# Order of issue alone: a planner that keeps VectorE and ScalarE apart by PSUM bank, with a newly searched table of ranks

## The chip, the core and the metric

The kernel runs on one core of one Trainium2 chip. The metric is device time in microseconds (us) of one execution, and less is better. The engines are TensorE (PE, with its weight loads as PEld), VectorE (DVE), ScalarE (ACT), GpSimd (POOL) and SyncE (SP), which here issues every DMA.

## The reference

The output is the sum of three terms for a sequence of S = 2048 tokens of width D = 576: the input itself, a spectral filter of the normalized input, and a mixture-of-experts layer with 64 experts, 32 heads and one choice in each head.

```
xn = layernorm(x)                                     # over the 576 columns
A  = irfft2(rfft2(xn) * (w_r + 1j * w_i))             # 2-D, over tokens and columns
q  = xn @ w_q                                         # 32 heads, 2 * 128 columns each
s1, s2 = q[..., :128] @ k1.T, q[..., 128:] @ k2.T     # 8 scores each
e  = argmax(s1) * 8 + argmax(s2)                      # one expert in each head
B  = sum over heads of gelu(xn . u[e]) * v[e]
out = x + A + B
```

A softmax over a single choice is 1, so the gate of the reference falls away.

## The kernel before

**The spectral branch.** Tokens are numbered n*16 + t, with n on the partitions. `ln(t, n)` normalizes blocks of tokens, `folds(t)` adds and subtracts mirrored columns on POOL and DVE, and `dft128(t)` does the transform of length 128 on PE. Its result is split into a high half in float16 (ACT copies it out of PSUM) and a residue (DVE subtracts the copy from the same PSUM data). The arrays `AB` and `ABL` hold both halves. Then sixteen frequency groups g pass through `d_fwd(g)` (columns), `s_fwd(g)` (length 16, two groups at a time), `s_mul(g)` (the filter, four products on DVE per pair, then POOL and ACT) and `s_inv(g)`, which writes `AB` and `ABL` again. `d_inv(t)` and `fin(t)` finish sixteen token blocks: `d_inv` brings the columns back (PE, then ACT's copy `es`, DVE's `eo`, and POOL's three operations that make `y`), and `fin` does the last length-128 transform plus the product with the experts' v on PE, adds the input on DVE and issues the store.

**The expert branch.** `fold_part(b, s)` multiplies the query weights by the keys while they stream in (32 loads of 576 KB into five buffers `w`), `fold_end` and `fold_last` turn the product into the tables `MU` and `MUL`. For eight blocks r of two token tiles, `x_t(r)` prepares the input, `scores(r)` multiplies it by `MU` and `MUL` (28 matmuls), `route(r)` finds the best choice of each head, and `combine(r)` makes the coefficients, which PE transposes and ACT copies into `CAT` for `fin`. `scores(r)` writes two PSUM banks, one for each token tile. ACT reads columns 448 to 511 of each bank for the gelu (two instructions named `act`), and DVE reads columns 0 to 447 of both banks for the maximum (`mx`) and for the comparison with it (the first write of a `w` buffer). So there ACT and DVE read the same banks, and neither needs the other's result. In `s_inv` ACT makes two copies (`AB` and `ABL`) from the same banks, and DVE's two residues each need one of them.

**What sets the order.** The kernel text is recorded, not issued: each call on an engine becomes an operation of a `_Plan`, with a cost from a table of formulas, a latency, and its dependencies. Up to 900 ns of matmuls of one stage on one PSUM tile are one operation. `forward` then plays a list scheduler: again and again it takes the engine that can start soonest, and on it, of the operations that can start at that time, the one with the smallest number in the table `RANK` (1308 numbers, one for each recorded operation). The same pass hands out PSUM banks to tiles, of which at most `LIMIT` of each kind are open at once. The resulting total order is the order in which the program is issued, engine by engine. The library below the kernel adds the semaphores: PSUM is one tensor called `banks`, and two instructions of different engines on the same bank are put one behind the other in the order in which they are issued, reads too. In the kernel before, the planner doesn't know of that last rule for two reads. [...]

Two more names occur below: `KP` is a small matrix of key differences that POOL makes from `kT` once at the start, and `rr` and `mv` hold the statistics of the normalization. `A` and `t` in the profile are the buffers of `folds` and `d_inv` (`A2_*`, `t1_*`), `yh` also that of `es`, and `MT` those of the routing. All engine calls go through one helper line, so that every row of the profile says L528; the changed file is ten lines longer, and the same helper is L538 there.

## Time and profile before

| | |
|---|---|
| times shown | 226.74, 227.78 and 229.1 us, median 227.78 us |
| profiled execution | span 226.4 us from its first to its last instruction; the page has no other time for it, so it stands 0.3 us below the fastest run shown and 1.4 us below the median |
| PE busy | 198.3 us (88%) |
| DVE busy | 195.3 us (86%) |
| POOL busy | 150.8 us (67%) |
| ACT busy | 135.2 us (60%) |
| DMA moved | 43.43 MB |

Times in the profile are in us unless ns is said. A row of the timeline has the start, the duration, the engine, the line, the operation, the names out<-in, the shape, the count of merged instructions, and in brackets the idle time of the engine before it with what ended it. A row of the view of waits has the waiting engine, what it waited for, and the total, the count and the longest. The view by windows has, for a stretch of the span, its length and then the busy time and count of PE, PEld, DVE, ACT and POOL, the granted PE clock, the DMA share and GB/s.

### The profile page before, as it was taken

To read this page: it belongs to the slowest core of one execution; us is meant where nothing else is said; L and a number is where in the kernel's file an instruction comes from. 1 tells how busy PE (TensorE), PEld (TensorE's weight loads), DVE (VectorE), ACT (ScalarE), POOL (GpSimd) and SP (SyncE) were. 2 spreads that over 40 slices of the span, in tenths; PEclk is the share of its full clock that TensorE was granted. 3 is DMA by queue.
4 is the path that set the end of the run, shared out by engine and by line. 5 is a ranking of instruction groups with operands and counts; after the bars stand their busy time and mean duration, and the time that the engine had idled before them with its cause. 6 is when DMAs were issued, how large, how long until landed. Compare 5 with 4: busy or idle time off the path is not lost.

```text
span 226.4 us, 5987 instructions
## 1 busy us (share of the span) xinstructions
PE 198.3 (88%) x2287; PEld 136.1 (60%) x2287; DVE 195.3 (86%) x423; ACT 135.2 (60%) x294; POOL 150.8 (67%) x217
## 2 busy tenths in 40 slices
PE   0197959999997999899888999999899999999984
PEld 0185536877675367584464665645566767788762
DVE  1979899997769789763999999999999999999843
ACT  2388877888397797949577577545483332242420
POOL 3889887842097829418668585459794977586880
PEclk9999999999999699999999999999999999999999
DMA  6999999979999995533334322200200002223234
GB/s 209 413 430 410 406 409 408 409 254 380 377 385 402 321 356 141 174 99 107 100 114 153 94 80 61 69 4 0 62 3 0 0 3 104 106 110 154 104 115 148
DMA packets 14572, 43.43 MB, mean 192 GB/s; under 512 B 1872, under 2 KB 4688, under 8 KB 14160
## 3 DMA queue, kind: packets, MB, share of 16 engines
q1 hardware_dynamic: 14544, 43.05, 52.0%
q8 instruction: 18, 0.29, 0.6%
q14 instruction: 10, 0.08, 0.1%
HBM read 38.33 MB, written 4.72 MB: 190 GB/s over the span
## 4 chain that ended last, share of the span: by engine, by line
PE 48%; DVE 34%; issue 7%; POOL 4%; ACT 4%; DMA 2%; DVEq 0%; ACTq 0%; POOLq 0%
PE banks L528 48%; DVE MT L528 8%; DVE w L528 6%; DVE t L528 6%; DVE XN L528 3%; POOL t L528 2%; DVE mx L528 2%; DVE A L528 2%; DVE AB L528 2%; DMA XN<-in_x_dram 2%; DVE st L528 1%; POOL A L528 1%; DVE ABL L528 1%; DVE rr L528 1%; ACT yh L528 1%
## 5 line engine op out<-in xcount | busy, mean ns | idle before, releaser
L528 PE MATMUL banks<-MU,xT 128*128 128x512 f16 x192 | 47.5, 379 | 1.1 <-DVE t L528 0.9
L528 POOL TENSOR_TENSOR xT<-xf,xT 128x512 f16<-128x512 f32 (+1 forms) x32 | 26.2, 819 | 16.6 <-ACT xT L528 14.2
L528 POOL TENSOR_TENSOR y<-t,t 128x289 f32<-128x289 f32 x32 | 22.6, 727 | 20.6 <-DVE t L528 20.3
L528 PE MATMUL banks<-c,AB 128*128 128x145 f16 (+1 forms) x384 | 35.2, 227 | 0.0
L528 POOL TENSOR_TENSOR A<-t 128x145 f32<-128x145 f32 (+2 forms) x48 | 31.2, 665 | 5.3 <-DVE t L528 3.1
L528 PEld LDWEIGHTS <-AB 128*128 128x128 f16 x384 | 32.2, 121 | 3.5 <-issue 1.4
L528 PEld LDWEIGHTS <-xT 128*128 128x128 f16 x224 | 20.6, 99 | 22.2 <-issue 2.1
L528 POOL TENSOR_TENSOR t<-XN 128x289 f32<-128x289 f32 x32 | 24.0, 770 | 8.8 <-DVE A L528 4.1
L528 ACT ACTIVATE yh<-banks,sc 128x580 f32<-128x580 f32 x16 | 11.9, 744 | 23.8 <-PE banks L528 16.9
L528 POOL TENSOR_TENSOR yh<-y,yh 128x578 f16<-128x578 f32 x16 | 21.9, 1377 | 5.4 <-ACT yh L528 4.5
L528 DVE SCALAR_TENSOR_TENSOR t<-banks,wx,Wt 128x578 f32<-128x578 f32 x32 | 24.1, 807 | 0.5 <-PE banks L528 0.4
L528 PE MATMUL banks<-A,c 128*128 128x288 f32 x64 | 21.8, 422 | 1.5 <-POOL A L528 0.9
L528 PE MATMUL banks<-Rs,yl 128*99 128x128 f32 x64 | 11.2, 305 | 13.5 <-ACT Rs L528 13.4
L528 PE MATMUL banks<-w,KP 128*32 128x288 f32 x256 | 22.0, 441 | 0.8 <-DVE mm__94 L528 0.8
L528 DVE TENSOR_TENSOR AB<-banks,AB 128x512 f16<-128x512 f32 x32 | 21.4, 675 | 1.3 <-ACT AB L528 0.7
L528 PE MATMUL banks<-c,ABL 99*128 99x289 f16 (+1 forms) x64 | 18.6, 291 | 1.4 <-DVE t L528 1.0
L528 ACT ACTIVATE AB<-banks 128x512 f16<-128x512 f32 x32 | 18.6, 587 | 2.0 <-PE banks L528 1.9
L528 PE MATMUL banks<-Rs,A 128*128 128x128 f32 x128 | 19.0, 298 | 0.0
L528 PEld LDWEIGHTS banks<-Rs,A 128*128 128x128 f32 x128 | 17.1, 209 | 2.5 <-issue 1.4
L528 PEld LDWEIGHTS banks<-Rs,yl 128*99 128x99 f32 x64 | 8.3, 180 | 16.6 <-ACT Rs L528 15.5
L528 DVE TENSOR_REDUCE MT<-w 128x128 bf16<-128x896 bf16 (+1 forms) x16 | 18.1, 1139 | 0.0
L528 ACT ACTIVATE ABL<-banks 99x256 f16<-99x256 f32 x32 | 12.0, 379 | 9.7 <-PE banks L528 9.6
(124 smaller groups left out, 433.3 us busy)
## 6 DMA issues: line engine op xcount, KB each, us to landing
w<-in_wq_dram SPq DMA_DIRECT2D x32, 576.0 KB, 7.0
xf<-in_xT_dram SPq DMA_DIRECT2D x16, 320.0 KB, 3.7
Wt<-in_W_dram SPq DMA_DIRECT2D x8, 578.0 KB, 6.1
out_dram<-XN SPq DMA_DIRECT2D x14, 288.0 KB, 2.1
XN<-in_x_dram SPq DMA_DIRECT2D x3, 1154.0 KB, 10.6
s<-in_s_dram SPq DMA_DIRECT2D x16, 192.0 KB, 3.4
XN<-in_x_dram SPq DMA_DIRECT2D x2, 577.0 KB, 4.6
c<-in_c_dram SPq DMA_DIRECT2D x1, 868.5 KB, 9.8
```

What stands on the lines that cost most here:

```text
L528: fn(*[x.place() if isinstance(x, _Ps) else x for x in args], **{k: x.place() if isinstance(x, _Ps) else x for k, x in kw.items()})
```

## The change

The change is to the planner and its table alone. No call in the body of the kernel is edited, so that each instruction of the program is issued as before, on the same engine, at another place.

Each operation outside PE now lists the PSUM banks of the tiles that it touches (`bk`). While it plans, `forward` keeps for each such bank the planned end of every access, with its engine (`seen`). An operation can start no sooner than the end of each earlier access of another engine to one of its banks. And the 1308 ranks are others. The old ranks were the positions of a finished order; the new ones are keys without such a trend, from which the scheduler makes an order.

```diff
 RANK = (
-    2, 13, 11, 15, 48, 86, 12, 14, 6, 4, 3, 5, 1, 53, 51, 54, 58, 7, 0, 8, 10, 9, 18, 21, 24, 20, 16, 23, 29,
...
+    115, 134, 157, 175, 296, 353, 133, 169, 298, 382, 628, 84, 987, 21, 253, 200, 170, 295, 126, 380, 249,
...
 class _Op:
     __slots__ = ("shape", "tiles", "eng", "calls", "cost", "lat", "deps", "succ", "stage", "pre", "port",
-                 "held", "opens", "after")
+                 "held", "opens", "after", "bk")
...
-            op.tiles, op.port = tiles, port
+            op.tiles, op.port, op.bk = tiles, port, []
...
             if isinstance(x, _Ps):
                 name = x.tile
+                if eng != "tensor":
+                    op.bk += [(name, int(b)) for b in np.flatnonzero(mask) if (name, int(b)) not in op.bk]
...
                 if o.port and port > t:
                     t = port
+                for b in o.bk:
+                    for x, u in seen.get(b, ()):
+                        if x != e and u > t:
+                            t = u
...
-        used, port = {k: 0 for k in LIMIT}, 0.0
+        used, port, seen = {k: 0 for k in LIMIT}, 0.0, {}
...
             if o.port:
                 port = free[e]
                 stale |= {"vector", "gpsimd"}
+            for b in o.bk:
+                seen.setdefault(b, []).append((e, free[e] + o.lat))
+                stale |= {"vector", "scalar"}
```

The sequence of stages stays what it was: a stage is at most some operations earlier or later on its engine. Three places show how it moved.

**ACT, around the gelu of the first block.** `xf` and `xT` belong to `x_t`, `t2` with `wm` to a load of filter weights, `A2` to `d_fwd`, `yh` and `yl` to `s_mul`, and `act_0` is the gelu of `scores(0)`, with the table load that it needs in front. Before:

```order
L528 ACTIVATE A2_2_100<-banks_66 128x578
L528 ACTIVATE A2_3_101<-banks_66 128x578
L528 ACTIVATE t2_0_106,wm_81<-Wt_2_113 128x1156
L528 ACTIVATE yh_1_137<-y_1_135 128x578
L528 ACTIVATE yh_0_136<-y_0_134 128x578
L528 ACTIVATE xT_1_92<-xf_0_123 128x640
L528 ACT_TABLE_LOAD
L528 ACTIVATE act_0_126<-banks_66,gs_88 128x64 x2
L528 ACTIVATE yl_1_105<-yh_1_137 128x396
L528 ACTIVATE xT_1_92<-xf_1_124 128x640
L528 ACTIVATE yl_0_104<-yh_0_136 128x396
```

And now:

```order
L538 ACT_TABLE_LOAD
L538 ACTIVATE act_0_126<-banks_66,gs_88 128x64
L538 ACTIVATE xT_1_92<-xf_0_123 128x640
L538 ACTIVATE t2_0_106,wm_81<-Wt_2_113 128x1156
L538 ACTIVATE A2_3_101<-banks_66 128x578
L538 ACTIVATE yh_0_136<-y_0_134 128x578
L538 ACTIVATE yh_1_137<-y_1_135 128x578
L538 ACTIVATE xT_1_92<-xf_1_124 128x640
L538 ACTIVATE yl_0_104<-yh_0_136 128x396
L538 ACTIVATE A2_2_100<-banks_66 128x578
L538 ACTIVATE yl_1_105<-yh_1_137 128x396
L538 ACTIVATE xf_0_123<-xf_0_123,bx_87 128x640
```

The table load and the first gelu now stand ahead of the other work of that place, and the second gelu, which followed the first at once, comes after the last row shown. In the order of the whole program the two used to stand on both sides of DVE's `mx`; now the first is ahead of it and the second behind both of DVE's reads.

**POOL, at the start of the program.** `t1` from `XN` and `A2` are the folds of the first token tiles, `rr` from `mv` their statistics, and `KP` from `kT` the key differences. Before:

```order
L528 TENSOR_TENSOR t1_0_96<-XN_67 128x289 x2
L528 TENSOR_TENSOR t1_1_97<-XN_67 128x289
L528 TENSOR_SCALAR rr_84<-mv_85 128x2
L528 TENSOR_TENSOR A2_0_98<-t1_0_96 128x145
L528 TENSOR_TENSOR t1_1_97<-XN_67 128x289
L528 TENSOR_TENSOR A2_1_99<-t1_1_97 128x145
L528 TENSOR_TENSOR KP_73<-kT_69 128x2x7 x4
```

And now:

```order
L538 TENSOR_TENSOR KP_73<-kT_69 128x2x7 x4
L538 TENSOR_TENSOR t1_0_96<-XN_67 128x289 x2
L538 TENSOR_TENSOR t1_1_97<-XN_67 128x289
L538 TENSOR_SCALAR rr_84<-mv_85 128x2
L538 TENSOR_TENSOR A2_0_98<-t1_0_96 128x145
L538 TENSOR_TENSOR t1_1_97<-XN_67 128x289
```

The four operations on `KP` moved ahead of the first folds. On the DMA queue the load of `kT` moved from third to second place, between the first two loads of `XN`.

**POOL, at the end of the program.** `t1` from `yh` is the first of the three operations of a `d_inv`, the two `A2` from `t1` are the others, and `MT` from `MT` is the low half of a block's coefficients in `combine`. Before:

```order
L528 TENSOR_TENSOR MT_79<-MT_79 128x2x64
L528 TENSOR_TENSOR A2_1_99<-t1_1_97 128x287
L528 TENSOR_TENSOR t1_0_96<-yh_0_136 128x2x144
L528 TENSOR_TENSOR A2_0_98<-t1_0_96 128x289
L528 TENSOR_TENSOR t1_1_97<-yh_1_137 128x2x144
L528 TENSOR_TENSOR A2_0_98<-t1_0_96 128x287
L528 TENSOR_TENSOR A2_3_101<-t1_1_97 128x287
L528 TENSOR_TENSOR t1_0_96<-yh_0_136 128x2x144
L528 TENSOR_TENSOR A2_3_101<-t1_1_97 128x289
L528 TENSOR_TENSOR A2_2_100<-t1_0_96 128x289
L528 TENSOR_TENSOR A2_2_100<-t1_0_96 128x287
```

And now:

```order
L538 TENSOR_TENSOR t1_0_96<-yh_0_136 128x2x144
L538 TENSOR_TENSOR MT_79<-MT_79 128x2x64
L538 TENSOR_TENSOR A2_0_98<-t1_0_96 128x287
L538 TENSOR_TENSOR A2_0_98<-t1_0_96 128x289
L538 TENSOR_TENSOR t1_1_97<-yh_1_137 128x2x144
L538 TENSOR_TENSOR MT_79<-MT_79 128x2x64
L538 TENSOR_TENSOR A2_3_101<-t1_1_97 128x287
L538 TENSOR_TENSOR t1_0_96<-yh_0_136 128x2x144
L538 TENSOR_TENSOR A2_3_101<-t1_1_97 128x289
L538 TENSOR_TENSOR A2_2_100<-t1_0_96 128x289
L538 TENSOR_TENSOR A2_2_100<-t1_0_96 128x287
```

The low halves of the last two blocks (6 and 7) now both fall among the last three `d_inv`; before, only that of block 7 came so late, and it was ahead of them. On PE the matmuls of the last `d_inv`, of tile 14, now stand ahead of both `fin(13)` and `fin(12)`, where they used to stand between the two.

129 rows, old and new, of the table RANK are left out of this document.

## Prediction

> **What bounds the kernel now.** I read the split into windows first, because the busy shares of the whole span (PE 88%, DVE 86%) hide that two engines take turns. Columns: length of the stretch, then busy time and count of PE, PEld, DVE, ACT and POOL, the granted clock, DMA.
>
> ```profile
> 0.00:10.00 10.00, 0.00 (x0) 0.00 (x0) 5.37 (x25) 2.14 (x4) 6.06 (x20) 1.00 0.82 296
> 10.00:32.00 22.00, 17.02 (x132) 12.64 (x132) 19.55 (x61) 19.10 (x57) 18.97 (x35) 1.00 1.02 416
> 32.00:68.00 36.00, 35.98 (x443) 26.83 (x447) 31.12 (x74) 27.26 (x64) 20.19 (x29) 1.00 0.97 370
> 68.00:105.00 37.00, 33.79 (x536) 22.47 (x529) 29.87 (x67) 29.48 (x59) 21.26 (x27) 0.95 0.71 240
> 105.00:152.00 47.00, 44.40 (x547) 26.06 (x546) 43.98 (x81) 29.99 (x59) 30.72 (x38) 1.00 0.28 84
> 152.00:210.00 58.00, 55.05 (x552) 39.04 (x550) 56.62 (x104) 23.70 (x50) 43.85 (x58) 1.00 0.15 53
> 210.00:226.40 16.40, 12.08 (x90) 9.04 (x89) 8.77 (x17) 3.55 (x7) 9.78 (x15) 1.00 0.34 127
> ```
>
> From 32 to 105 PE is the bound: it is idle for 0.02 + 3.21 us there, and DVE, with 12.0 us idle, has room. From 105 to 210 DVE is idle for only 3.02 + 1.38 = 4.4 us, so it is the bound there. At the start and in the last 16 us neither is full; there a chain of single steps sets the pace. An order of issue can't remove work, so all that this change can win lies in idle time: 5.0 us of PE from 10 to 32, 3.2 us to 105, 4.4 us of DVE to 210, and a few tenths in the tail.
>
> Next I read the view of waits, for the waits that only a shared PSUM bank can cause, and the timeline where they are longest.
>
> ```profile
> DVE ABL L528 <- ACT AB L528: 2.3, 2, 1.9
> DVE mx L528 <- ACT act L528: 2.3, 1, 2.3
> DVE AB L528 <- ACT ABL L528: 0.4, 1, 0.4
> DVE w L528 <- ACT act L528: 0.3, 1, 0.3
> ACT act L528 <- DVE mx L528: 1.9, 2, 1.2
> ```
>
> A residue `ABL` needs ACT's copy `ABL`, not its copy `AB`; the maximum `mx` needs nothing of the gelu `act`. All five rows are pairs of reads. The total is 5.3 us on DVE and 1.9 us on ACT, though the first row holds some waiting for true needs as well, because ACT makes the two copies one behind the other.
>
> ```profile
> 104.70 0.28 DVE L528 TENSOR_REDUCE mxr<-banks 1x1 f32<-1x128 f32 x1 [1.18 <-PE banks L528]
> 104.85 0.73 ACT L528 ACTIVATE xT<-xf 128x640 f16<-128x640 f32 x1
> 105.59 1.28 ACT L528 ACT_TABLE_LOAD   x1
> 106.88 0.31 ACT L528 ACTIVATE act<-banks,gs 128x64 f32<-128x64 f32 x1
> 107.23 1.09 DVE L528 TENSOR_REDUCE mx<-banks 128x128 f32<-128x896 f32 x1 [2.25 <-ACT act L528]
> 108.36 0.31 ACT L528 ACTIVATE act<-banks,gs 128x64 f32<-128x64 f32 x1 [1.16 <-DVE mx L528]
> 108.70 1.09 DVE L528 TENSOR_TENSOR w<-banks,mx 128x896 bf16<-128x896 f32 x1 [0.32 <-ACT act L528]
> 109.15 0.54 PE L528 MATMUL banks<-s,yl 64*99 64x128 f16 x12 [0.98 <-ACT yl L528]
> ```
>
> This is the one place where it hurts. ACT comes late to the first gelu, loads its table for 1.28 us, and then DVE and ACT take turns on the two banks: DVE waits 2.25, ACT 1.16, DVE 0.32. ACT's `yl`, queued behind the second gelu, is late for that, and PE waits 0.98 us for it.
>
> **The change, part by part.** Nothing is removed or added, so each term is a stall that goes or comes.
>
> *The gelu of scores(0).* The table load and the first gelu stand now ahead of four to six other ACT operations, and the second gelu behind both of DVE's reads. So the load falls into a time when ACT would wait for PE, and the turn-taking ends: up to 2.25 + 0.32 us of DVE's idle time and 1.16 us of ACT's. But `mx` also needs the last matmul of scores(0), and in the new order eight matmuls of scores(1) stand ahead of the last eight of scores(0). By the row below eight take 1.89 us.
>
> ```profile
> 105.50 1.89 PE L528 MATMUL banks<-MU,xT 128*128 128x512 f16 x8
> ```
>
> So DVE gets a new wait, on PE, of most of that size; these eight matmuls are work that PE need not do later. What is surely won is the 0.98 us that PE lost for `yl`, and about half a microsecond of DVE. I take -1.5 us. Bounds: -2.6 (both DVE waits gone and nothing in their place) and +0.5 (the 1.89 us less the 1.4 us that the rest gives back).
>
> *The residues of s_inv.* Three waits of this kind are seen, one per row.
>
> ```profile
> 98.27 0.42 DVE L528 TENSOR_TENSOR ABL<-banks,ABL 33x256 f16<-33x256 f32 x1 [1.93 <-ACT AB L528]
> 132.84 0.42 DVE L528 TENSOR_TENSOR ABL<-banks,ABL 33x256 f16<-33x256 f32 x1 [0.34 <-ACT AB L528]
> 169.20 0.69 DVE L528 TENSOR_TENSOR AB<-banks,AB 128x512 f16<-128x512 f32 x1 [0.41 <-ACT ABL L528]
> ```
>
> The first lies where PE is the bound and costs nothing. The other two lie where DVE is: 0.34 + 0.41 = 0.75 us. Nearly all these pairs keep their order (ACT's two copies, then DVE's residues), so only what stands between them can help. I take -0.65; bounds 0 and -0.75.
>
> *The start.* On POOL the four small operations on `KP` move ahead of the first folds, and `kT` moves up one place on the DMA queue.
>
> ```profile
> 4.92 2.20 POOL L528 TENSOR_TENSOR t<-XN 128x289 f32<-128x289 f32 x3 [3.19 <-DMA XN<-in_x_dram]
> 9.26 0.85 POOL L528 TENSOR_TENSOR KP<-kT 128x14 f32<-128x14 f32 x4
> 6.50 0.80 DVE L528 BATCH_NORM_STATS2 st<-XN 128x6 f32<-128x288 f32 x2
> 7.28 0.80 DVE L528 BATCH_NORM_STATS2 st<-XN 128x6 f32<-128x288 f32 x2
> 10.45 0.96 PE L528 MATMUL banks<-Rs,yl 128*99 128x128 f32 x3 [10.45 <-ACT Rs L528]
> DMA to landing us min/median/max: 4.9/4.9/4.9
> ```
>
> The last row is that of `kT`; issued at 1.64, it lands at 6.5, behind two loads of `XN`. Behind one of them I estimate it for 5.0, just after the first `XN` (at which the first row starts, 4.9). So POOL begins its folds at 5.0 + 0.85 = 5.9, about 0.9 us later. On the other side DVE's statistics of the next two token tiles, 1.6 us in two rows, now stand behind the first fold, so that DVE is ready earlier and POOL's chain is what remains: the first matmul at about 9.9 instead of 10.45. From 10 to 32 DVE, ACT and POOL are all at 19 to 19.6 of 22 us, and what was put behind the first fold is due there. I take -0.2; bounds +0.9 (kT lands late and all of it carries) and -0.6.
>
> *The end.* The last rows of POOL and what waits behind them:
>
> ```profile
> 218.42 0.70 POOL L528 TENSOR_TENSOR t<-yh 128x288 f32<-128x288 f32 x1 [0.66 <-ACT yh L528]
> 219.08 1.98 POOL L528 TENSOR_TENSOR A<-t 128x289 f32<-128x289 f32 x3
> 219.82 0.75 PE L528 MATMUL banks<-A,c 128*128 128x288 f32 x2 [0.93 <-POOL A L528]
> 223.04 0.52 DVE L528 SCALAR_TENSOR_TENSOR XN<-banks,sc,XN 128x288 f32<-128x288 f32 x1 [0.21 <-PE banks L528]
> ```
>
> POOL's last chain is the bound, and it waits once, 0.66 us, for ACT's copy of the last `d_inv`. Its matmuls now stand ahead of both `fin(13)` and `fin(12)`, where a `fin` is two halves of the 0.75 us and more that the PE row shows, so that copy comes over a microsecond earlier and POOL runs through. The low half of block 6 moves into the tail, but from POOL's own queue just ahead of it, where it made room; block 7's goes behind a fold and has microseconds until `fin(15)` asks for it. I take -0.6; bounds -0.66 and +0.4 (the moved half stands in the chain).
>
> *Everything else.* Most operations of DVE have moved by a few places. I have no row that prices this, and take 0. The bounds are half of DVE's 4.4 us idle between 105 and 210 won, or as much lost: -2.2 and +2.2. One more doubt is not of the order: the window from 68 to 105 shows a granted clock of 0.95, so up to 0.05 * 37 = 1.9 us of PE time there came from a slow stretch that another execution may have elsewhere or not at all.
>
> The sum is -1.5 - 0.65 - 0.2 - 0.6 = -2.95 us, made against the span of 226.4: 223.45. The median shown is 227.78, 1.4 above that span, and I carry this distance over: 224.8 us, 1.3% below the median.
>
> **The rivals.** *The stall only changes its partner.* PE is the bound until about 105, so DVE's wait for ACT becomes the wait for the scores(1) matmuls, and the 0.98 us on PE come back where another late copy holds it. For it speaks that DVE's idle 1.18 us at 104.70 is already a wait on PE. Against it speaks that ACT is relieved as well. Then the first term is +0.3, and the sum -0.65 - 0.2 - 0.6 + 0.3 = -1.15: 226.6 us.
>
> *The change doesn't do what it says.* The plan's costs are formulas; where ACT runs late against them, the pairs collide again. Nearly all residues keep ACT's second copy ahead of them. Then only the tail moves: 227.78 - 0.6 = 227.2 us.
>
> *DVE and POOL collide more: slower.* Some DVE operations on SBUF take far longer at some places than at others, in the same form:
>
> ```profile
> L528 DVE TENSOR_TENSOR w<-w,wt x8: 607/610/1697, 109.8 to 190.0; 128x896 bf16<-128x896 bf16 x8
> L528 DVE TENSOR_TENSOR w<-MT,iv x8: 407/411/1519, 117.6 to 203.3; 128x512 bf16<-128x512 bf16 x8
> 109.83 1.60 DVE L528 TENSOR_TENSOR w<-w,wt 128x896 bf16<-128x896 bf16 x1
> 109.79 1.92 POOL L528 TENSOR_TENSOR xT<-xf,xT 128x512 f16<-128x512 f32 x2 [0.59 <-ACT xT L528]
> L528 DVE TENSOR_TENSOR w<-w,wt 128x896 bf16<-128x896 bf16 x8 | 7.0, 870 | 0.0
> L528 DVE TENSOR_TENSOR w<-MT,iv 128x512 bf16<-128x512 bf16 x8 | 5.0, 628 | 0.0
> ```
>
> The minimum is 607 ns and the mean 870; the one of 1.60 us begins 0.04 us behind a POOL operation of about the length that it is too long by. These two groups lose 8 * (0.870 - 0.607) + 8 * (0.628 - 0.407) = 3.9 us now, all of it where DVE is the bound. If the new order meets POOL twice as often it loses another 3.9, and from 2.95 us up that decides: at three times, +7.8 - 2.95 = +4.85, it is 227.78 + 4.85 = 232.6 us; at twice, 228.7. For it speaks that both engines were reordered throughout and that a new search need not find the old gaps again. [...]
>
> [...]
>
> **How the numbers follow.** The forecast, 224.8 us, gets 0.58. Its own range, 222.6 to 227.0, is 224.8 with the 2.2 us of the unpriced moves to either side; of the 0.58, 0.12 lies less than 1% below the median. The changed partner (226.6) gets 0.16, of which 0.02 end slower; the change without effect (227.2) 0.07; more collisions 0.19, of which 0.06 stay within 1% and 0.13 don't. That makes 0.46 faster by over 1%, 0.39 within 1%, and 0.15 slower; about 1% is what a measurement of this kernel, with 226.74 to 229.1 in three runs, can tell from no change. For 8 in 10 the range is 221.6 (the good bounds of the four terms, -4.6, half of the unpriced -2.2, and 0.5 of the 1.9 us of the clock: 227.78 - 6.2) to 229.5 (between the collisions at twice and at three times).
>
> **What would show it.** Right: `mx` of the first block no longer waits for `act` but for PE, by less than 2.5 us; the table load comes before 104; the rows of waits between `ABL`, `AB`, `mx` and `act` shrink below 2 us in all; POOL's last chain has no wait for `yh`; the first matmul comes between 9.5 and 10.5; DVE is idle for less than 4 us between 105 and 210. Wrong: DVE's busy sum above 199 us (collisions with POOL), PE idle for over 4 us between 32 and 105, or a first matmul after 11.

## The result and the profile after

The change made the kernel a little slower: 229.54 us, median of 20 runs (227.21 to 231.36), against 227.34 us of before, median of 20 runs on the same chip (226.44 to 229.33). The ratio is 1.0076 with a 95% interval of 1.0049 to 1.0103, so 1.7 us lost (1.1 to 2.3). The forecast was 224.8 us. In three kernels below (`start_after_rest_before`, `dma_order_alone`, `first16_after`) the profiled execution ran at a mean granted clock of 0.852, 0.672 and 0.857, against 0.983 to 1.000 in their other runs, so their profiles are not read, and all ratios leave such runs out.

The profiled execution of the change took 227.71 us (span 225.9), near the fast end of its twenty. Read alone, it would tell of no loss; what it shows is where time moved. In the runs on record the time is 1.7 to 2.1 us longer than the span, mostly 1.8 or 1.9, so the profiled execution of before, with a span of 226.4, belongs to a time of some 228.2 us: it is not a fast one, as the table before the prediction has it. The forecast doesn't change by that, since 1.4 us carried over from the span lead back to the median. The view by windows, with the same columns as in the prediction:

```profile
0.00:10.00 10.00, 0.00 (x0) 0.00 (x0) 4.82 (x18) 2.36 (x5) 6.04 (x20) 1.00 0.78 273
10.00:32.00 22.00, 13.66 (x100) 10.97 (x104) 19.55 (x58) 15.75 (x45) 15.53 (x31) 0.88 0.97 390
32.00:68.00 36.00, 35.55 (x393) 25.80 (x389) 31.04 (x72) 24.98 (x64) 17.88 (x28) 0.98 0.91 336
68.00:105.00 37.00, 33.42 (x589) 24.06 (x582) 31.20 (x73) 31.83 (x64) 23.81 (x28) 1.00 0.78 283
105.00:152.00 47.00, 46.87 (x546) 28.38 (x545) 43.54 (x84) 34.03 (x67) 34.95 (x43) 1.00 0.32 97
152.00:210.00 58.00, 55.45 (x587) 39.66 (x586) 57.24 (x105) 23.44 (x47) 40.87 (x58) 1.00 0.14 51
210.00:225.90 15.90, 11.26 (x86) 8.28 (x84) 10.13 (x18) 3.49 (x7) 9.33 (x15) 0.96 0.35 131
```

Count PE's matmuls: from 10 to 32 there are 100, where before had 132, and by 68 it is 493 against 575. From 68 to 105 the lag shrinks (589 against 536), and by 210 it is gone (2215 against 2210; each is the sum of the rows from 10 to 210). So the start lost and the rest won it back. ACT and POOL, at 19 us of 22 in the second window before, are at 15.75 and 15.53 now: they were idle more. DVE is busy for 19.55 us in both, but with 58 instructions instead of 61. PE's timeline shows where it starved:

```profile
14.34 0.68 PE L538 MATMUL banks<-Rs,yl 128*99 128x128 f32 x4 [1.13 <-ACT yl L538]
20.15 2.03 PE L538 MATMUL banks<-Rs,yl 128*99 128x128 f32 x8 [3.12 <-ACT Rs L538]
24.52 1.66 PE L538 MATMUL banks<-w,KP 128*32 128x288 f32 x24
29.93 1.81 PE L538 MATMUL banks<-Rs,yl 128*99 128x128 f32 x8 [3.75 <-ACT Rs L538]
```

PE waits 3.12 and 3.75 us for `Rs`, ACT's scaled copy of the transform matrix, which needs the normalization of its token tile. And each stretch is followed by a stretch at half clock. In the view by windows, with the borders at the switches of the clock (seventh number):

```profile
16.54:19.96 3.42, 0.48 (x8) 0.00 (x0) 3.38 (x10) 2.64 (x9) 2.24 (x5) 1.00 0.98 405
19.96:23.37 3.41, 3.22 (x15) 3.22 (x16) 3.16 (x10) 2.62 (x8) 1.99 (x5) 0.50 1.03 414
23.37:30.20 6.83, 3.08 (x37) 1.98 (x37) 5.78 (x19) 5.29 (x15) 4.37 (x9) 1.00 0.92 350
30.20:33.61 3.41, 3.41 (x20) 2.22 (x19) 1.92 (x7) 2.59 (x8) 3.10 (x6) 0.50 0.44 169
```

Twice, for 3.41 us each, the clock is 0.50, directly behind a window in which PE did little: 0.48 us in the first row, and 0.27 us in the last 3.41 of the third. A third such stretch begins at 224.75, 1.1 us before the end. The profile of before has one, at 74 (0.51 from 74.0 to 77.5). One is worth 0.5 * 3.41 / 226 = 0.0075 of the mean clock, and so the twenty runs of the change sort themselves: three at 0.991 to 0.992 (median 228.1 us), fifteen at 0.982 to 0.985 (229.9) and two at 0.975 to 0.978 (230.7). The windows are only a part of the spread: the fifteen alone run from 227.67 to 231.36 us.

### The profile page after: what moved, and what is told of

Same layout as the page of the kernel before. It is cut to its first block, busy times and chain, and to the rows that moved or that the text cites. A ratio compares the mean times of both kernels' runs of the same rounds, so it can differ in the third digit from the quotient of the medians.

```text
span 225.9 us, 5983 instructions
## 1 busy us (share of the span) xinstructions
PE 196.2 (87%) x2287; PEld 137.1 (61%) x2287; DVE 197.5 (87%) x423; ACT 135.9 (60%) x294; POOL 148.4 (66%) x217
## 4 chain that ended last, share of the span: by engine, by line
PE 56%; DVE 27%; POOL 6%; issue 4%; DMA 3%; ACT 2%; SPq 0%; POOLq 0%; DVEq 0%; ACTq 0%
PE banks L538 56%; DVE t L538 5%; DVE MT L538 4%; DVE A L538 3%; DVE w L538 3%; DVE AB L538 3%; DMA kT<-in_kT_dram 2%; POOL xT L538 2%; POOL yh L538 1%; DVE mx L538 1%; DMA s<-in_s_dram 1%; DVE ABL L538 1%; DVE st L538 1%; DVE rr L538 1%; DVE sc L538 1%
## 5 line engine op out<-in xcount | busy, mean ns | idle before, releaser
L538 PE MATMUL banks<-MU,xT 128*128 128x512 f16 x192 | 46.6, 379 | 0.6 <-DVE AB L538 0.6
L538 POOL TENSOR_TENSOR xT<-xf,xT 64x128 f16<-64x128 f32 (+1 forms) x32 | 26.4, 829 | 12.8 <-ACT xT L538 9.1
L538 PEld LDWEIGHTS <-AB 128*128 128x128 f16 x384 | 31.7, 122 | 2.8 <-issue 1.2
L538 POOL TENSOR_TENSOR y<-t,t 128x289 f32<-128x289 f32 x32 | 22.1, 709 | 16.1 <-DVE t L538 14.0
L538 PE MATMUL banks<-Rs,yl 128*99 128x128 f32 x64 | 12.1, 330 | 18.6 <-ACT Rs L538 17.2
L538 POOL TENSOR_TENSOR yh<-y,yh 128x578 f16<-128x578 f32 x16 | 22.4, 1417 | 4.0 <-ACT yh L538 3.9
L538 PEld LDWEIGHTS banks<-Rs,yl 128*99 128x99 f32 x64 | 9.1, 197 | 21.8 <-ACT Rs L538 18.7
L538 PE MATMUL banks<-w,KP 128*32 128x288 f32 x256 | 20.3, 422 | 0.3 <-DVE t L538 0.3
L538 ACT ACTIVATE xf<-xf,bx 128x640 f32<-128x640 f32 x16 | 13.1, 829 | 7.9 <-DMA xf<-in_xT_dram 7.9
```

The costliest lines, as they stand in the source:

```text
L538: fn(*[x.place() if isinstance(x, _Ps) else x for x in args], **{k: x.place() if isinstance(x, _Ps) else x for k, x in kw.items()})
```

## The experiments

The instructions are the same in all kernels but one (which adds matmuls to fill PE's idle time), so an experiment is an order. In eighteen kernels the table of ranks holds positions, and the planner takes only the next operation in that order on each engine; its times still hand out the PSUM slots. At 50 us of the plan the two orders have issued the same operations but one; at 28.7, 94 and 194 us but three at most. There they can be cut and joined. Ratios are to before, run on the same chip beside each kernel; 0.01 is 2.3 us. Differences in us between kernels are taken from these ratios.

### Where: cutting the order

**Start of before, rest of the change.**

```diff
-            for i in wait[e]:
-                if pre[i]:
+            for i in wait[e]:
+                if pre[i] or i != seq[e][done[e]]:
...
-order = order of the change
+order = first 375 of before, then what is left, as in the change
```

> The first 50 us of the plan (375 instructions) in the order of before, all that follows in the order of the change; at this cut the two orders have issued the same instructions. Theory S (the start loses, by starved TensorE and the clock that falls with it; the middle gains about 2 us as far as forecast): 225.4 us, between 224.5 and 226.3, so below both kernels. Rival M (the start is neutral, the loss lies behind it in VectorE and GpSimd getting in each other's way): 229.5, as the change. Rival X (no part is responsible, the two only suit or do not suit each other): neither, about 228.

Measured: 223.28 us, ratio 0.9797 (0.9764 to 0.9830). That is 4.6 us below before and 6.3 below the change, the fastest of all kernels here; below it is called the good hybrid. Theory S holds in its sign, but the time lies below its range: the rest won 4.6 us and not about 2.

```profile
10.00:32.00 22.00, 17.01 (x134) 12.78 (x135) 19.55 (x60) 18.79 (x56) 19.07 (x34) 1.00 1.02 416
32.00:68.00 36.00, 36.00 (x403) 26.31 (x401) 29.71 (x68) 26.40 (x60) 18.94 (x28) 0.95 0.94 361
68.00:105.00 37.00, 33.43 (x562) 23.43 (x561) 31.27 (x72) 31.13 (x63) 23.73 (x30) 1.00 0.71 253
105.00:152.00 47.00, 46.87 (x577) 28.79 (x576) 45.94 (x87) 32.39 (x65) 34.72 (x43) 1.00 0.30 89
```

PE, ACT and POOL are back at their busy times of before from 10 to 32, and from 105 to 152 PE is busy for 46.87 us as in the change, where before had 44.40.

**The reverse.**

```diff
-order = order of the change
+order = first 374 of the change, then what is left, as before
```

> The reverse: the first 50 us of the plan in the order of the change, then the order of before. Theory S: 231.2 us, between 230.0 and 232.5, slower than both kernels. Rival M: 227.3, as before. Together with the first hybrid the two differences should add up to that of the whole change, +2.2 us, if nothing is carried across the cut.

Measured: 234.44 us, ratio 1.0278 (1.0245 to 1.0312). The two differences add up: -0.0203 + 0.0278 = +0.0075, and the whole change is +0.0076. So nothing is carried across the cut that these intervals (about a microsecond for each difference) would show: the start costs 6.3 us and the rest wins 4.6. Rivals M and X fall. The time lies above the range of theory S, since the start costs more than it took.

**Only the first 28.7 us.**

```diff
-order = order of the change
+order = first 202 of the change, then what is left, as before
```

> Only the first 28.7 us of the plan (202 instructions) in the order of the change. Theory S, since both idle stretches of TensorE (3.12 and 3.75 us, both ended by Rs) are set by what VectorE and ScalarE issue there: 230 to 232 us, nearly all of the loss of the start. If the loss of the start lies between 28.7 and 50: 227.3. Rival M: 227.3.

Measured: 232.80 us, ratio 1.0218 (1.0186 to 1.0249): 5.0 of the 6.3 us, a little above the range of theory S.

**Only the first 16 us, from both sides.**

```diff
-order = order of the change
+order = first 100 of the change, then what is left, as before
```

> Only the first 100 instructions (16 us of the plan) in the order of the change, the rest in the order of before (ten instructions are issued by only one of the two at this cut). Theory E (early: loads, KP and statistics of the first four tokens carry the loss, what follows only inherits it): 231.5 to 232.8 us, as with 28.7 us of the change. Theory W (the loss is made on the way: the change's order loses more at each wait between 16 and 28 us, the order of before makes lateness good again): 229.3 us, between 228.3 and 230.3.

Measured: 230.51 us, ratio 1.0153 (1.0120 to 1.0185), 3.5 us.

```diff
-order = order of the change
+order = first 100 of before, then what is left, as in the change
```

> The reverse: the first 100 instructions in the order of before, the rest in the order of the change. Theory E: 223.3 to 224.5 us. Theory W: 227.5 us, between 226.5 and 228.5, with an idle stretch of TensorE of more than 2 us left ahead of 32 us.

Measured: 226.33 us, ratio 0.9956 (0.9928 to 0.9984). That lies 2.7 us below the change and 3.6 above the good hybrid. Neither theory holds alone: about half of the loss is made in the first 16 us, half behind it, and the second half has its own stall, PE's longest:

```profile
18.08 1.12 PE L534 MATMUL banks<-Rs,yl 128*99 128x128 f32 x8 [1.01 <-ACT Rs L534]
27.47 2.03 PE L534 MATMUL banks<-Rs,yl 128*99 128x128 f32 x8 [4.02 <-ACT Rs L534]
```

**The rest, cut at 94 and at 194 us.**

```diff
-order = order of before
+order = first 664 of before, then what is left, as in the change
```

> The first 664 instructions (94 us of the plan) in the order of before, the rest in the order of the change; both orders have issued exactly the same instructions at this cut. The gain of 4.4 us that the order of the change has behind 50 us is split: by the forecast's terms (gelu of scores(0) 1.5, residues of s_inv 0.65, tail 0.6) 2.75 us lie behind this cut, so 224.8 us, between 224.0 and 225.6. If the surplus also lies behind it: 223.3. If the gain lies mostly ahead of it, in the stage that waits for TensorE: 226.5 to 227.5.

```diff
-order = order of before
+order = first 1223 of before, then what is left, as in the change
```

> Only what the plan issues behind 194 us (85 instructions, the last tokens) in the order of the change. Forecast's term for the tail: 0.6 us, so 226.9 us against 227.5 of before, between 226.3 and 227.5. Rival: the end is set by TensorE's remaining work and the last store, and nothing is gained: 227.5.

Measured: 223.95 us, ratio 0.9833 (0.9796 to 0.9871), and 226.16 us, ratio 0.9925 (0.9897 to 0.9953). So from 194 on 1.7 us are won, from 94 to 194 2.1, and from 50 to 94 0.8, the last with intervals that overlap. The subtraction at 194 takes for granted that the tail is worth the same behind either order, and no pair of kernels tests that. Both times lie below the ranges expected. Joined to the order of before, the tail won nearly three times its forecast. POOL's last rows in `after_from_194`:

```profile
213.85 0.70 POOL L526 TENSOR_TENSOR t<-yh 128x288 f32<-128x288 f32 x1
214.50 0.43 POOL L526 TENSOR_TENSOR MT<-MT 128x128 f16<-128x128 f32 x1
214.89 0.69 POOL L526 TENSOR_TENSOR A<-t 128x287 f32<-128x287 f32 x1
215.53 0.69 POOL L526 TENSOR_TENSOR t<-yh 128x288 f32<-128x288 f32 x1
216.19 1.99 POOL L526 TENSOR_TENSOR A<-t 128x289 f32<-128x289 f32 x3
```

No row waits for `yh`, as foreseen. Not foreseen was the rest: before, PE had two breaks behind 205 (0.22 us for DVE's `XN` and 0.93 for POOL's `A`), and here its timeline has none over 0.1 us from there to its end. In the change itself the tail does not run through. PE breaks off twice, for 0.33 us (POOL's `A`) and here:

```profile
215.01 0.28 PE L538 MATMUL banks<-id,MT 128*128 128x128 f16 x2 [0.96 <-POOL MT L538]
```

That is the low half of a block's coefficients, which the new order puts behind a fold: POOL writes it at 214.53 us, and the chain that ended last runs through it. The good hybrid and `after_from_94` have the same two breaks (0.33 and 0.96 us, 0.34 and 0.95). So the 1.7 us are the tail's price behind the order of before, and what it is worth in the change isn't measured.

**The gelu alone.** Two instructions are moved in the order of before, on ACT (the first by three places; the expectation miscounts):

```diff
 load_w(8)
+scores(0) act, first tile
 s_mul(7) yh, s_mul(6) yh, x_t(3)
-scores(0) act, first tile
-scores(0) act, second tile
 s_mul(7) yl, x_t(3), s_mul(6) yl
+scores(0) act, second tile
```

> The order of before with two instructions moved on ScalarE: the first gelu of scores(0) four places earlier, the second behind the last read of the bank by VectorE, as the change has them. Forecast's term: 1.5 us gained, so 226.0 us, between 225.4 and 226.6. Rival: the turns of the two engines at the bank are only put elsewhere (VectorE's maximum or ScalarE's next copies wait instead), 227.5 or above.

Measured: 225.58 us, ratio 0.9935 (0.9907 to 0.9964), 1.5 us won. The forecast's first term holds in size, for these two instructions alone:

```profile
103.91 1.28 ACT L526 ACT_TABLE_LOAD   x1
105.21 0.31 ACT L526 ACTIVATE act<-banks,gs 128x64 f32<-128x64 f32 x1
105.73 1.09 DVE L526 TENSOR_REDUCE mx<-banks 128x128 f32<-128x896 f32 x1 [0.66 <-PE banks L526]
106.85 1.09 DVE L526 TENSOR_TENSOR w<-banks,mx 128x896 bf16<-128x896 f32 x1
109.17 0.30 ACT L526 ACTIVATE act<-banks,gs 128x64 f32<-128x64 f32 x1
```

`mx` begins at 105.73 instead of 107.23 and waits for PE, not for `act`, and the two reads of DVE follow each other without a turn of ACT between them. The change itself moves more of ACT's queue: there the table load (at 104.46), the first gelu, `xT` and a load of filter weights also stand ahead of a copy `A2` of `d_fwd`, and DVE, which no longer waits for `act`, waits for that copy:

```profile
108.42 0.76 DVE L538 TENSOR_TENSOR A<-banks,A 128x578 f16<-128x578 f32 x1 [2.48 <-ACT A L538]
```

Before, DVE had done these subtractions from 102.11 on without a wait. PE is busy for 46.87 of the 47 us from 105 to 152 in the change, so the 0.98 us that it lost for `yl` have not come back.

### How much of it is the clock

```diff
     def dft128(t):
         F, FL, Rs = FF.pop(t)
         p = PS("x")
+        for k in range(WARM.get(t, 0)):          # WARM = {2: 16, 4: 16}
+            P.matmul(p[:, k % 2, 0:128], idn, idn, start=True, stop=True)
```

> The change's order with sixteen matmuls of a constant ahead of dft128(2) and sixteen ahead of dft128(4), put into a PSUM tile that is overwritten afterwards: they fill some 2.1 us of each idle stretch of TensorE, and what is computed stays the same. Theory C (a good part of the loss is the half clock that follows the idle stretches): no window of half clock at 20 and 30 us, granted clock 0.99 or more, 227.8 us, between 227.0 and 228.6. Rival I (the waiting alone costs, the clock does not): 229.5 or, if the added matmuls hold up real ones, above it.

Measured: 227.33 us, ratio 0.9987 (0.9957 to 1.0017), 2.0 us below the change (0.0089 of ratio, with both intervals give or take 0.9 us). The only addition is work, and the kernel is faster for it. The windows of the profile, the first three with the same borders as above (the added matmuls count too, as 32 rows in each stretch):

```profile
16.54:19.96 3.42, 3.42 (x35) 3.03 (x28) 3.38 (x10) 2.64 (x9) 2.24 (x5) 1.00 1.00 417
19.96:23.37 3.41, 3.41 (x34) 3.29 (x32) 3.41 (x11) 3.09 (x9) 2.48 (x6) 1.00 1.02 412
23.37:30.20 6.83, 6.81 (x73) 5.41 (x72) 6.69 (x20) 5.81 (x18) 5.05 (x9) 1.00 1.00 367
10.00:32.00 22.00, 20.54 (x184) 17.24 (x184) 20.43 (x60) 16.94 (x49) 16.56 (x33) 1.00 0.99 390
```

No window of half clock is left, and theory C holds: half clock behind the idle stretches costs, and about 2.0 us come back without it. That is no exact share of the 6.3. The added matmuls run for 3.84 us in each stretch, longer than expected, and hold the first real ones behind them up (20.61 us instead of 20.15); and the good hybrid, against which the 6.3 us are counted, has one window of half clock itself (0.91 from 32 to 50 us). The waiting is the larger part in any case: this kernel never falls to half clock there and is still 4.3 us slower than the good hybrid (3.3 to 5.3).

### Which instructions

**The scaling of ln(4,4).** The second stretch waits for the `Rs` of token tile 4, whose scaling DVE does behind the statistics of later tiles.

```diff
 DVE  ln(4,4) reciprocal
+DVE  ln(4,4) scaling, three steps
 DVE  ln(8,4) statistics ... ln(12,4) statistics
-DVE  ln(4,4) scaling, three steps
```

> The change's order with eight instructions moved forward: the three scaling steps of ln(4,4) on VectorE from behind the statistics of ln(8,4) and ln(12,4) to right behind their reciprocal, and the steps of folds(4) and folds(5) that wait for them (one on GpSimd, one on VectorE, yl and Rs on ScalarE). Theory L (these late steps make the second idle stretch of TensorE, 3.75 us ended by Rs at 29.9, and the half clock behind it): Rs of folds(4) by 24 us instead of 29.5, the second stretch under 1 us, 226.8 us, between 225.6 and 228.0. Rival N (something else would have been late there anyway, such as the statistics on ScalarE or the rows of x): the stretch stays above 2.5 us and the time is 229.5.

Measured: 230.49 us, ratio 1.0109 (1.0072 to 1.0147). `Rs` of tile 4 did come at 24.88 instead of 29.47, the second stretch is gone, and nothing is won, since new ones stand behind it:

```profile
24.88 0.39 ACT L534 ACTIVATE Rs<-c,rr 128x128 f32<-128x128 f32 x1
25.65 0.40 ACT L534 ACTIVATE Rs<-c,rr 128x128 f32<-128x128 f32 x1
```

```profile
32.71 0.68 PE L534 MATMUL banks<-Rs,yl 128*99 128x128 f32 x4 [2.06 <-ACT Rs L534]
35.08 0.37 PE L534 MATMUL banks<-c,bx 128*1 128x128 f32 x1 [1.69 <-DVE AB L534]
```

Theory L was right on the wait and wrong on the price. The stall travelled on, to the next `Rs` (tile 6) and to DVE's residue `AB`, and behind it the clock is at one half for two windows, from 33.70 on (0.81 from 32 to 50 us).

**The loads.** kT moved ahead of the second load of `XN`, and so did `c32`, which the prediction had not looked at.

```diff
 SP  XN(0,1)
-SP  XN(2,3)
 SP  kT
 SP  c32
+SP  XN(2,3)
```

On the good hybrid (this and the other loads of the first 50 us as in the change). D and V are its two theories:

> The hybrid that took 223.3 us (start of before, rest of the change) with one thing more from the change: the order in which SP issues the loads of the first 50 us. In the change kT and c32 go ahead of XN(2,3), which lands at 8.19 us instead of 6.31, and XN(4..7) at 11.13 instead of 9.88. Theory D (the late tokens are what costs the start): between 226.0 and 228.5 us, 227.3 taken, since 1.3 to 1.9 us are late and one or two windows of half clock may follow. Theory V (the order on the engines costs, above all that VectorE has the statistics of ln(2,2) behind the first folds; the loads do not): 223.3 to 224.2.

Measured: 225.27 us, ratio 0.9881 (0.9828 to 0.9934), 1.9 us above the hybrid (with both intervals 0.5 to 3.3) and between the ranges of the two theories: the loads cost, but less than theory D took. On the change's order, the load alone moved back:

> The change's order with one load moved: XN(2,3) back in front of kT and c32, as before the change. Theory D: 226 us, between 225.3 and 227.5. Theory V: no change, 229.5, since VectorE takes up these tokens at 10.4 us and they have landed by 8.2 in any case.

Measured: 230.55 us, ratio 1.0106 (1.0051 to 1.0161): no gain, as theory V had it, but for another reason. It is in POOL's first rows, of the change and then of this kernel:

```profile
5.00 0.72 POOL L538 TENSOR_TENSOR KP<-kT 128x14 f32<-128x14 f32 x4 [3.15 <-DMA kT<-in_kT_dram]
5.68 2.20 POOL L538 TENSOR_TENSOR t<-XN 128x289 f32<-128x289 f32 x3
```

```profile
6.83 0.72 POOL L534 TENSOR_TENSOR KP<-kT 128x14 f32<-128x14 f32 x4 [4.97 <-DMA kT<-in_kT_dram]
7.51 2.21 POOL L534 TENSOR_TENSOR t<-XN 128x289 f32<-128x289 f32 x3
```

With `KP` first on POOL, the folds wait for `kT`. What `XN(2,3)` wins, 1.9 us, the first fold loses (7.51 against 5.68). The first matmul comes at 12.16 us instead of 10.34. The two pieces of the change hang together.

**Load and KP, both back.**

```diff
 SP   XN(0,1)
+SP   XN(2,3)
 SP   kT
 SP   c32
-SP   XN(2,3)
-POOL KP, four operations
 POOL folds(0), folds(1)
+POOL KP, four operations
```

> The change's order with two places put back: XN(2,3) is loaded ahead of kT and c32, and on GpSimd the four operations on KP stand behind folds(1) instead of ahead of folds(0), so that nothing there waits for kT (with the load alone the first folds had to wait for kT until 6.8 us). Theory K (load and KP hang together, and each alone only exchanges one late operand for the other): first fold at 4.9 us instead of 5.7, first matmul near 9.6 instead of 10.3, 228.3 us, between 227.0 and 229.0. Theory V (the place of the statistics on VectorE and ScalarE decides, whatever lands when): 229.5 or above.

Measured: 227.22 us, ratio 0.9984 (0.9958 to 1.0010), 2.1 us below the change. Theory K holds, at the good end of its range: the first matmul starts at 9.45. But the stretches of 2.56 and 3.75 us ahead of 20.50 and 30.39 are still there:

```profile
9.45 1.18 PE L534 MATMUL banks<-Rs,yl 128*99 128x128 f32 x4 [9.45 <-ACT Rs L534]
20.50 1.83 PE L534 MATMUL banks<-Rs,yl 128*99 128x128 f32 x8 [2.56 <-ACT Rs L534]
30.39 1.58 PE L534 MATMUL banks<-Rs,yl 128*99 128x128 f32 x8 [3.75 <-ACT Rs L534]
```

**KP and kT alone, on the good hybrid.**

```diff
 SP   XN(0,1)
+SP   kT
 SP   XN(2,3)
-SP   kT
+POOL KP, four operations
 POOL folds(0), folds(1)
-POOL KP, four operations
```

> The good hybrid with the four operations on KP ahead of the first folds on GpSimd and kT loaded ahead of XN(2,3); c32 and the other loads stay. By the forecast's sizes the first folds start 0.75 us later: 223.3 + 0.75 = 224.0, between 223.5 and 224.6. If kT alone pushes XN(2,3) back by more than a microsecond: 225 or above. If GpSimd's chain has slack: 223.3.

Measured: 224.50 us, ratio 0.9862 (0.9820 to 0.9905), 1.5 us above the hybrid (0.3 to 2.7). The time lies in the range expected, and 0.75 us is not excluded.

**The statistics of ln(2,2).** Before, DVE made them while it waited for the first square root; in the change they stand behind the first folds. On the good hybrid:

```diff
 DVE  ln(0,2) statistics
-DVE  ln(2,2) statistics
 DVE  folds(0), folds(1)
+DVE  ln(2,2) statistics
```

> The good hybrid (223.3 us: start of before, rest of the change) with the statistics of ln(2,2) moved behind the first folds on VectorE, its square root behind yl(1) on ScalarE and its scaling behind ABL of dft128(1), as the change has them. Theory V: 225.3 us, between 224.5 and 226.5. Rival: the feed has slack there and nothing changes, 223.3 to 223.9.

Measured: 223.48 us, ratio 0.9833 (0.9799 to 0.9867): 0.8 us by the ratios, 0.2 by the medians, and the intervals overlap widely. Theory V falls: this was the piece that I suspected most. DVE's busy sum rose to 198.3 us in this kernel, 3.1 above the hybrid, and it cost hardly anything.

**The feed moved forward by hand.** These steps and those of ln(4,4) moved forward on the change's order: with the load put back, without it, and with load and `KP` put back.

```diff
 DVE  ln(0,2) statistics
+DVE  ln(2,2) statistics
 DVE  folds(0), folds(1)
-DVE  ln(2,2) statistics
+DVE  ln(2,2) scaling; folds(2), folds(3)
...
 DVE  ln(4,4) reciprocal
+DVE  ln(4,4) scaling
```

> The change's order with XN(2,3) in front and with the feeding steps forward: the statistics of ln(2,2) on VectorE into the wait for the first square root, its scaling behind the first folds, folds(2) and folds(3) as early as their operands allow, and the eight moves of the last set for ln(4,4). Theory V: first Rs of token 2 by 17 us instead of 19.7, no idle stretch of TensorE over 2 us ahead of 30, 225 us, between 223.5 and 226.5. Theory D: no better than with the load alone. If the stalls only travel on, as they did with ln(4,4) alone: 228 to 230.

> The same moves on the engines without the load: XN(2,3) stays behind kT and c32. VectorE's statistics of ln(2,2) then stand ahead of the first fold and wait for tokens that land at 8.2 us. Theory V: 225.5, a little above the kernel with both. Theory D, and likewise if both are needed together: 229.5 or above, since what was moved ahead now waits for the load and holds the first folds up.

> Both together: load and KP put back, and the feeding steps of tokens 2 to 5 forward on VectorE, ScalarE and GpSimd. K and V together: idle stretches of TensorE ahead of 35 us not longer than before the change (1.9 us), 224.5 us, between 223.3 and 226.5. If the stalls travel on to the tokens behind (8 to 15), which stay in the change's order: 227.5 to 230.

Measured: 230.60 us, ratio 1.0141 (1.0078 to 1.0205); 230.21 us, ratio 1.0113 (1.0077 to 1.0149); 229.86 us, ratio 1.0086 (1.0053 to 1.0118). None comes near the 225 us that theory V asked for. The second and the third lie where their rivals had them, the first 0.6 us above. The last is even 2.3 us slower than load and `KP` back alone. As with ln(4,4), the stalls moved: in the first two the first matmul came at 11.97 and 12.10 us instead of 10.34, and in the third PE waits 2.47 us for `yl` at 15.97, 2.25 for `Rs` at 33.47 and 1.68 for `AB` at 35.83. Which step held up which was not followed.

### Plan and chip

What both orders were made for is the plan's own clock. These are the starts that the planner computed, in us, beside those of the profile:

```
                 first fold     Rs of tile 0    Rs of tile 2    Rs of tile 4
                 plan  chip     plan  chip      plan  chip      plan  chip
before           4.7   4.9      9.5   10.0      18.0  18.3      22.2  22.5
the change       4.9   5.7      8.9    9.9      17.3  19.7      25.4  29.5
```

The order of before runs 0.2 to 0.5 us behind its plan. The order of the change begins 0.8 us late and is 4.1 us late at tile 4. One place where it falls behind can be read from DVE's rows of the change:

```profile
8.12 0.15 DVE L538 SCALAR_TENSOR_TENSOR rr<-rr 128x2 f32<-128x2 f32 x1
8.38 0.60 DVE L538 SCALAR_TENSOR_TENSOR A<-t,rr 128x145 f32<-128x145 f32 x1
8.91 0.65 DVE L538 SCALAR_TENSOR_TENSOR rr<-rr 128x2 f32<-128x2 f32 x1
9.48 0.98 DVE L538 SCALAR_TENSOR_TENSOR A<-t,rr 128x145 f32<-128x145 f32 x1
```

The first and the third are the same operation on the same shape, 0.15 and 0.65 us; the second and the fourth are one form too, 0.60 and 0.98, and 0.39 to 0.40 us before the change. The long ones lie beside POOL's folds, which run from 8.38 on almost without a break. They add up: DVE's busy sum is 197.0 to 198.1 us in the six kernels that begin in the order of the change, and 194.1 to 195.8 in the six that begin in that of before (of the profiles that are read, without the moved statistics and steps). That these lengths make the lag is argued from the rows; no run took them away, and the kernel with late statistics, at 198.3 us, speaks against the sum alone.

## Why the prediction was wrong, point by point

- **The start, the step that failed.** It read: "I take -0.2; bounds +0.9 (kT lands late and all of it carries) and -0.6", and it cost +6.3 us. I priced it at the first matmul, which came at 10.34 against 9.9 forecast and 10.45 before, inside the range named. But the first matmul isn't what the start delivers: it delivers sixteen `Rs` one after the other, the last at 54.79 us instead of 49.57, and on the way the order of the change starved PE by 3.12 and 3.75 us. The sentence ahead of the price said that DVE, ACT and POOL are at 19 to 19.6 of 22 us and that what is put behind the first fold is due there. That was the warning, and the bound did not follow it. I also looked at `kT` and not at what it was moved past: `XN(2,3)` landed 6.1 us behind an issue at 2.09, so at 8.2, where it had been 6.3.
- **The clock.** I took the half clock at 74 us as a doubt of one execution ("may have elsewhere or not at all"). But 82 of the 95 runs of before that stand beside the experiments show 0.991 or 0.992, one such window each, and filling two idle stretches of the change took its windows away and won 2.0 us (1.1 to 2.9). So in these runs it followed PE's idle time, and the order has a hand in it.
- **The gelu, right where it is moved alone.** -1.5 forecast, -1.5 measured alone (-0.8 to -2.1). In the change the new wait of `mx` for PE is 0.79 us, below the 1.89 allowed, but DVE's 2.48 us for `A` stand beside it, a wait that the forecast did not look for. The table load came at 104.46 and not ahead of 104. What the term is worth in the change isn't measured by itself.
- **The residues, not separated.** -0.65 forecast. Behind 94 and ahead of 194, 2.1 - 1.5 = 0.6 us are left for them and all else, with intervals of about a microsecond, if gelu and tail keep their prices there.
- **The end, right in sign, mis-sized.** -0.6 forecast, -1.7 measured behind the order of before (-1.1 to -2.3). I priced POOL's wait for `yh` alone. By the chain that ended last, before also hangs on DVE and ACT between 202 and 210 us, and `after_from_194` on PE but for one copy. In the change the risk that I had bounded with +0.4, the moved half in the chain, did come: 0.96 us of PE.
- **Everything else**, 0 forecast: -0.8 us between 50 and 94, not certain.
- **The sum without the start**: -2.75 forecast, -4.6 measured. The forecast was wrong by its sign because of one term.
- **The rivals.** The changed partner came half true: DVE's wait for `act` is gone, and a wait of 2.48 us for another copy of ACT has come, but PE's 0.98 us did not come back. That the change does nothing is refuted by the gelu. Collisions, the rival on the slower side, got the sign right and the place wrong. The two groups that it priced became shorter, while others of the same form grew, most of all in the middle `MT<-mx,MT` (from 2.2 to 4.5 us) and at the start `A<-t`:

```profile
L538 DVE TENSOR_TENSOR w<-w,wt 128x896 bf16<-128x896 bf16 x8 | 5.6, 703 | 0.0
L538 DVE TENSOR_TENSOR w<-MT,iv 128x512 bf16<-128x512 bf16 x8 | 3.4, 426 | 0.0
L528 DVE TENSOR_TENSOR A<-t 128x288 f32<-128x288 f32 x16 | 7.3, 462 | 0.7 <-POOL t L528 0.7
L538 DVE TENSOR_TENSOR A<-t 128x288 f32<-128x288 f32 x16 | 9.0, 574 | 0.6 <-POOL t L538 0.4 <-PE banks L538 0.2
```

  The first two took 7.0 and 5.0 us before, so they won 3.0 us, and yet DVE's sum rose from 195.3 to 197.53 us, below the 199 that I named. In the good hybrid `A<-t` is at 7.3 us and the sum at 195.2, so the surplus belongs to the start. What it costs there is open (see Plan and chip).
- **The signs named in advance.** PE idle for over 4 us between 32 and 105 was one for "wrong", and it stands at 0.45 + 3.58 = 4.03. That was the only one of the three to speak, and by a hair, because I put the window behind the place of the loss. The matmul count from 10 to 32, 100 against 132, would have told it at once. Of the signs for "right", the first matmul, `mx` and POOL's last chain came as named, and the five rows of waits that the prediction shows are gone (`AB` waits 2.7 us, but for the copy that it needs). DVE's idle time from 105 to 210 is 105 - 43.54 - 57.24 = 4.2 us and not below 4, and the table load was late.

Two things stay open. About 3 us of the start's loss are made between 16 and 50 us of the plan (2.8 by the one pair of kernels, 3.6 by the other), and no single step was found that carries them: the scaling of ln(4,4), moved alone, passed its stall on, and so did the sets of steps. And the prices of the pieces taken singly on the good order (loads 1.9, `KP` with `kT` 1.5, statistics 0.8, each give or take more than a microsecond) aren't a sum, since the first two share the early `kT`.

The version that beats both kernels is the hybrid: 223.28 us, 2.0% below before (1.7 to 2.4).

## What to carry to other kernels

When an order changes everywhere, price a start-up phase by what it must deliver until the bound engine runs full, not by its first delivery, and read every queue for what was moved back, not only for what was moved forward. Two orders of the same instructions can be cut where both have issued the same set and joined crosswise: two kernels then tell which part wins and which loses, and the better parts may make a third order that beats both. At the start, where DVE, ACT and POOL of before are busy for 19 to 19.6 of 22 us, four kernels with steps moved by hand passed their stalls on (ratios of 1.0086 to 1.0141, against 1.0076 of the change), while the whole start of before brought 0.9797. Here whole stretches of an order that is known to run were the safer unit.

## What the runs showed of the hardware that was not expected

**The clock.** In the profiled executions of before and of the change, the granted clock stood at one half from 74.05 to 77.47 us (before), and from 19.96 to 23.37, from 30.20 to 33.61 and from 224.75 to the end (the change). Each stretch that ended lasted 3.413 us, and from the start of one to the start of the next in the change it is 10.24 and 194.55 us, 3 and 57 times that. I worked out PE's busy time in each window of 3.41 us on this grid, from the window of the first matmul on. Half clock followed the window with 1.47 us busy before (from 70.64) and those with 0.48, 0.27 and 1.21 us in the change (from 16.54, 26.78 and 221.34). Of the windows at full clock that full clock followed, the least busy had 1.66 and 1.75 us before (from 19.44 and 29.68) and 1.86 and 1.85 us in the change (from 74.57 and 84.81). Idle stretches ahead of half clock were also shorter than a window: 3.12 us in the change, and at most 2.38 us (up to 23.61) in the kernel with late statistics, with a granted clock of 0.86 from 20 to 32. Counted from the first instruction, the first border of the grid lies at 2.37 us before and at 2.89 in the change. Whether this place makes the one to three stretches of one program's runs (0.992 to 0.975 in the change) isn't shown.

The granted clock doesn't account for every slow matmul. In the change eight matmuls of one form (`Rs,A`) took 1.91 us at 11.30 and 1.06 us at 14.86, with a granted clock of 1.00 from 10 to 15 and from 15 to 20. What made the first eight slow isn't shown.

**A small load ahead of a large one.** With `kT` (8 KB) and `c32` (192 KB) ahead of it, `XN(2,3)` (577 KB) landed 1.9 us later, at 8.2 instead of 6.3. SP's rows of the change show half of that:

```profile
1.16 0.42 SPq L538 DMA_DIRECT2D kT<-in_kT_dram  x1
1.63 0.42 SPq L538 DMA_DIRECT2D c<-in_c_dram  x1
2.09 0.43 SPq L538 DMA_DIRECT2D XN<-in_x_dram  x1
```

The load is issued 0.92 us later, at 2.09 instead of 1.17, since the two issues ahead of it take SP 0.42 us each, with 0.05 and 0.04 us behind them. And it takes 6.1 us to land instead of 5.1. With `kT` alone ahead of it (`kp_first`) it is issued at 1.64 and lands 5.1 us later, 0.4 us late.
